# Linear attention followed by an MLP on one core: centring with the norm weight folded elsewhere, and matmuls on zeros in planned gaps of TensorE

## The chip, the cores and the metric

The kernel runs on one core of a Trainium2 chip. The metric is device time in microseconds (us) of one execution; lower is better. Four timed runs of the kernel before gave a median of 379.74 us (379.36 to 380.61). A core has the engines TensorE (PE: matmuls and weight loads), VectorE (DVE), ScalarE (ACT), GpSimd (POOL), and queues that issue transfers; SyncE (SP) here only issues transfers. Each engine works through its own instructions in order and waits at the head of its queue. Matmul results land in PSUM, of which this kernel uses eight banks.

## The reference

Shapes: q, k, v are 8 batches x 8 heads x 576 rows x 64 columns; w_phi is 64 x 128; the MLP is 512 -> 2048 -> 512.

```python
def phi(x):
    proj = np.einsum('bhsd,df->bhsf', x, w_phi)
    proj = proj - np.max(np.abs(proj), axis=-1, keepdims=True)
    return np.concatenate([np.exp(proj), np.exp(-proj)], axis=-1)
q_p, k_p = phi(q), phi(k)
kv = np.einsum('bhsf,bhsd->bhfd', k_p, v)
z = np.sum(k_p, axis=2)
num = np.einsum('bhsf,bhfd->bhsd', q_p, kv)
den = np.einsum('bhsf,bhf->bhs', q_p, z)[..., None] + 1e-06
# then, with the heads joined to x of 8 x 576 x 512:
mu = np.mean(x, axis=-1, keepdims=True)
var = np.mean((x - mu) ** 2, axis=-1, keepdims=True)
xn = (x - mu) / np.sqrt(var + 1e-06) * g_ln
out = x + np.maximum(xn @ w_ch1, 0.0) @ w_ch2
```

The MLP has no bias and a ReLU, so the positive factor 1/sqrt(var) of a row can be applied after the second matmul, and the kernel does that.

## The kernel before

The eight batches are four pairs. A pair has 1152 rows: nine tiles of 128 rows, in three groups r = 0, 1, 2 of three tiles. Attention runs in 32 units of two (batch, head) combinations, eight units a pair. In pair 0 units 0 to 3 finish batch 0 and units 4 to 7 batch 1; group r = 0 needs units 0 to 3 only.

One unit on the engines: transposes of k and q (L542; for later pairs a DMA transpose, L524), products with w_phi (`pm`, L572), row maxima on DVE (`m`, L592), exponentials on ACT (`EB`, L623), the product for the transposed features of q (`pt`, L670) with its exponentials (`ea`, L676), scaling of v on POOL (`vv`, L637 to L646), the sums over rows (`kv`, L696 and L701), numerator and denominator (`num`, L730), their scaling on DVE (L736 to L748) and the division on POOL, which writes the MLP's input x (L754).

The MLP for a group: row statistics on DVE (L873, L874), centring to `xc` (L881 on DVE, or the two steps L887 and L891 on POOL), a transpose to `xT` (pair 0: twelve TensorE transposes at L938, copied out of PSUM by L948; later pairs: DMA transposes, L923), the first matmuls (`hT_ps`, L989, four of 384 columns for each of 16 slices of 128 hidden columns), ReLU on ACT or DVE (L999, L997), the second matmuls (`ch_ps`, L1021), and scaling plus residual on DVE (L1029). The first `ch_ps` of pair 0 waits for all of w2.

Nothing of the order is fixed by loops. `Order` holds every operation with a rank, an estimated duration on each engine that may do it, what it reads and writes, and the PSUM banks it takes. `due` works backwards for due times; `run` simulates the engines with these estimates, gives each operation to an engine, and emits it into that engine's instruction list in that order. A change of a duration or of the allowed engines can thus reorder everything.

Two queues matter below. SP issues, in order, the loads of q, k, v and of g_ln; for pair 1 they begin with the row remainders `kx`, ahead of which POOL clears one small column (`kx1` memset, L1181), and all later loads of q, k and v stand behind these. POOL issues the loads of w1 and w2, two at a time, each pair of loads after the `vv` of units 2, 3, 5 and 6 (`WEIGHTS`, L1154).

Of the kernel before, what the change touches and what calls it, by code (L numbers as in the profile page):

```python
# [24 lines left out]


STAY = 10.0


class Op:  # L30
    __slots__ = (
        "alts", "emit", "rank", "lag", "users", "acquire", "release",
        "ready", "left", "number", "rows", "taken", "at", "early",
    )


class Order:
# [73 lines left out]
    def run(self):  # L111
        waiting, free, room, events, done = {}, {}, self.room, [], []
        rows = False

        def offer(op):
            heapq.heappush(events, (op.ready, 1, op.number, op, None))

        for op in self.ops:
            for engine in op.alts:
                waiting.setdefault(engine, [])  # L120
                free.setdefault(engine, 0.0)
            if not op.left:
                offer(op)
        now = 0.0
        while events:
            now = events[0][0]
            while events and events[0][0] <= now + 1e-9:
                _, kind, _, op, _ = heapq.heappop(events)
                if kind == 1:
                    for engine in op.alts:  # L130
                        key = op.ready if engine in ("DMA", "CAST") else op.rank
                        heapq.heappush(waiting[engine], (key, op.number, op))
                elif kind == 0:
                    for name, n in op.release or ():
                        room[name] += n
            for engine, queue in waiting.items():
                if free[engine] > now + 1e-9 or not queue:
                    continue
                passed, held, op = [], set(), None
                if engine == "PE" and rows:  # L140
                    near = sorted(i for i in queue if i[2].rows and not i[2].taken)
                    near = [i for i in near if room[i[2].acquire[0]] >= i[2].acquire[1]]
                    if near and near[0][0] < queue[0][0] + STAY:
                        op = near[0][2]
                while queue and op is None:
                    item = heapq.heappop(queue)
                    op = item[2]
                    if op.taken:
                        op = None
                        continue  # L150
                    if op.acquire is None or (
                        op.acquire[0] not in held and room[op.acquire[0]] >= op.acquire[1]
                    ):
                        break
                    held.add(op.acquire[0])
                    passed.append(item)
                    op = None
                for item in passed:
                    heapq.heappush(queue, item)
                if op is None:  # L160
                    continue
                op.taken, op.at = True, (now, engine)
                if op.acquire:
                    room[op.acquire[0]] -= op.acquire[1]
                us = op.alts[engine]
                if engine == "DMA" and free.get("CAST", 0.0) > now:
                    shared = free["CAST"] - now
                    us = 4.0 * us if 4.0 * us <= shared else us + shared * 0.75
                end = now + us
                if engine == "PE" and op.rows != rows:  # L170
                    rows = op.rows
                    end += 0.1
                lag = LAG[engine] if op.lag is None else op.lag
                free[engine] = end
                done.append((op, engine))
                heapq.heappush(events, (end, 2, op.number, op, None))
                heapq.heappush(events, (end + lag, 0, op.number, op, None))
                for o in op.users:
                    same = len(o.alts) == 1 and engine in o.alts
                    o.ready = max(o.ready, end + (0.1 if same else lag))  # L180
                    o.left -= 1
                    if not o.left:
                        offer(o)
        assert len(done) == len(self.ops)
        for op, engine in done:
            if op.emit:
                op.emit(engine)
        return now

# [2 lines left out]
def kernel(  # L192
# [45 lines left out]
    ps_B = ctx.enter_context(tc.tile_pool(name="ps_B", bufs=8, space=bass.MemoryType.PSUM))  # L238

    wphi_f = consts.tile([P, F], FP32, name="wphi_f")  # L240
    gln_sb = consts.tile([P, DM], FP32, name="gln")
    ident = consts.tile([P, P], BF16, name="ident")
    wbq = consts.tile([P, 2, F], BF16, name="wbq")
    wbk = consts.tile([P, 2, F], BF16, name="wbk")
    eps_sb = consts.tile([P, 1], FP32, name="eps")
# [32 lines left out]
    def add_any(alts, rank, emit, **kw):  # L278
        ahead_of = early(kw)
        sched.add(alts, rank, emit, early=ahead_of, **kw)  # L280

    def mm(n, cols):
        return n * (cols / 2.4 + 3.5) / 1000.0
# [102 lines left out]
    def load_w2(n, rank, after):  # L386
# [4 lines left out]
            r=after, w=[("w2", jj) for jj in range(j0, j1)],  # L391
        )

    def tails(g, V, qheads, with_k, slot):
# [19 lines left out]
        def products():  # L416
            pool, tag, _ = bank(g)
            j["px"] = ps = pool.tile([P, 1024 if tag == "A" else 512], FP32, tag=tag, name="px")
            for i, what in enumerate(parts):
                nc.tensor.matmul(  # L420
                    ps[:, i * 2 * F : (i + 1) * 2 * F], j["T"][:, i * P : (i + 1) * P],
                    wbk if what == "k" else wbq, start=True, stop=True,
                )
# [139 lines left out]
    def a_main(u, V, sides):  # L563
        n, g = u["n"], u["g"]

        def products(i):
            for e in range(2):
                u["pm", i, e] = ps_B.tile([P, MX // 2, F], FP32, tag="B", name="pm")
            for c in range(4):
                for e in range(2):  # L570
                    rows = slice(e * D, (e + 1) * D)
# [89 lines left out]
    def a_feat(u, V):  # L661
        n = u["n"]

        def products():
            u["EA"] = ea_bufs[n % NE]
            for e in range(2):
                u["pt", e] = ps_B.tile([P, 512], FP32, tag="B", name="pt")
            for e in range(2):
                rows = slice(e * D, (e + 1) * D)
                nc.tensor.matmul(  # L670
# [17 lines left out]
    def a_kv(u, V):  # L688
        n, g, uu = u["n"], u["g"], u["uu"]

        def products(t):
            EB, vv = u["EB"], u["vv"]
            if t == 1:
                u["kv"] = ps_B.tile([P, 2, 2, D1], FP32, tag="B", name="kv")
            ps = u["kv"]
            nc.tensor.matmul(  # L696
                ps[:, t, :, :], u["EBx"][:, t, uu, :], vv[:, t, MX : MX + 2, :],
# [20 lines left out]
    def a_num(u, V, chunks, em_of, puts, r):  # L718
# [4 lines left out]

        def products():
            st["ps"] = ps = ps_B.tile([P, 2, nch, D1], FP32, tag="B", name="num")
            for t in range(2):
                for i, terms in enumerate(chunks):
                    terms = terms(t)
# [133 lines left out]
    def x_stats(pr, r, V):  # L862
# [4 lines left out]
        for i, t in enumerate(ts):  # L867
# [8 lines left out]
            def center(e, i=i, t=t):  # L876
                if ("xc", r) not in pr:
                    pr["xc", r] = moe_sb.tile([P, NM, DM], BF16, tag="xc", name="xc")
                xc = pr["xc", r][:, i, :]
                if e == "DVE":  # L880
                    nc.vector.scalar_tensor_tensor(  # L881
                        out=xc, in0=x[:, t, :], scalar=pr["mv"][:, t, 0:1],
                        in1=gln_sb, op0=ALU.subtract, op1=ALU.mult,
                    )
                else:
                    xd = moe_sb.tile([P, DM], FP32, tag="xd", name="xd", bufs=1)
                    nc.gpsimd.tensor_tensor(  # L887
                        out=xd, in0=x[:, t, :], in1=bcast(pr["mv"][:, t, 0], 1, DM),
                        op=ALU.subtract,
                    )  # L890
                    nc.gpsimd.tensor_tensor(out=xc, in0=xd, in1=gln_sb, op=ALU.mult)  # L891

            w = [("mv", pair % 2, t)]
            if r == 0 and i == 0:
                w = [("mv", pair % 2, i_) for i_ in range(NT)]
            add("DVE", 0.72, V, stats, r=[("x", pair % NX, t, h) for h in range(H)], w=w)
            add_any({"DVE": 0.62, "POOL": 2.1}, V, center, r=["gln"] + [("mv", pair % 2, t)] + [("x", pair % NX, t, h) for h in range(H)],
                    w=[("xc", slot, i)])
            V += 1.0

# [9 lines left out]
    def x_trans(pr, r, slot_c, V):  # L910
# [20 lines left out]
        for k0 in range(0, KC, 2):  # L931
# [11 lines left out]
            def copy(e, k0=k0, st=st):  # L943
                if ("xT", r) not in pr:
                    pr["xT", r] = moe_sb.tile(
                        [P, KC, RN], BF16, tag="xT", name="xT", bufs=NXT
                    )
                copy_on(  # L948
                    e, pr["xT", r][:, k0 : k0 + 2, 0:cols],
                    st["ps"][:, 0 : 2 * cols].rearrange("p (k n) -> p k n", k=2),  # L950
                )

            key = ("xT_ps", pr["pair"], r, k0)
            wk = [("xT", slot, k0, i) for i in range(NM)]
            add("PE", mm(2 * n, 128), V, products, r=[("xc", slot_c, i) for i in range(n)],
                w=[key, *wk], acquire=("B", 1))
            add_any({"DVE": 0.08 + 0.128 * n, "ACT": 0.12 + 0.21 * n}, V, copy, r=[key], w=wk,
                    release=[("B", 1)])


# [17 lines left out]
    def moe(pr, V):  # L978
# [4 lines left out]
        def first(r, jj, V):  # L983
            st, cols = {}, len(tiles[r]) * P

            def products():
                st["ps"] = ps_B.tile([P, RN], FP32, tag="B", name="hT_ps")
                for kc in range(KC):
                    nc.tensor.matmul(  # L989
                        st["ps"][:, 0:cols], w1_sb[:, kc, jj * P : (jj + 1) * P],  # L990
# [133 lines left out]

    make_identity(nc, ident)
    nc.scalar.preload_act_table_set("natural_log_exp_and_others")
    for t_ in (wbk, wbq):
        nc.vector.memset(t_, 0.0)
    nc.vector.memset(eps_sb, 1e-6)
    for vx in vx_bufs:  # L1130
        nc.gpsimd.memset(vx, 0.0)
# [10 lines left out]
    for e_ in range(2):  # L1142
        add("DVE", 0.4, 0.0, lambda e=e_: phi_blocks(e), r=[("wphi", e_)], w=["wb"])

    dma("SP", 3.0, 262144, gln_sb, dram(moe_g_ln, 0, [[0, P], [1, DM]]), w=["gln"])
    load_main(k, 2, [0, 1], "SP", 3.0)
    load_main(q, 2, [0, 1], "SP", 3.1)
    load_tails(k, 0, [1], "SP", 3.2)
# [6 lines left out]
    for n in range(NU + 2):  # L1155
# [51 lines left out]
        if 0 < n <= NU:  # L1207
# [11 lines left out]
            if i == H - 1:  # L1219
                pr["V"] = V + 0.9 * step  # L1220
                ahead[0] = E_MOE
                moe_V = moe(pr, moe_V)
            ahead[0] = E_ATT
        gs = []
        if n % HG == 1 and n // HG + 3 != NGRP:
# [46 lines left out]
```

## Time and profile before

| What | us |
|---|---|
| median of the timed runs | 379.74 |
| the profiled execution's own time | 382.27 |
| span of its instructions | 380.5 |
| PE busy | 350.5 |
| DVE busy | 274.8 |
| ACT busy | 251.9 |
| POOL busy | 207.8 |
| first matmuls L989, x768 | 150.3 |
| second matmuls L1021, x551 recorded | 141.4 |
| centring: L881 on DVE x19 | 20.2 |
| centring: L887 + L891 on POOL x17 | 18.8 + 22.7 |
| load of g_ln: issued at 11.97, landed at | 19.54 |

The profile page gives busy times of each engine and the span in 40 slices of 9.5 us, each with a digit for the busy tenths. The row PEclk is the share of TensorE's full clock that was granted. Its records begin at 23.43 us; ahead of that the row shows full clock for want of a record. A window row lists, for one stretch, the busy time and the number of instructions of PE, PE weight loads, DVE, ACT and POOL, then the granted clock, the DMA share and GB/s. A timeline row gives start and duration, the engine, line and tiles, the number of merged instructions, and in brackets the idle time before it and what ended it. Matmuls overlap in the pipeline, so a row's duration holds the drain of its last matmul.

### The profile page before, as it was taken

The page shows a single profiled execution, that of the slowest core. Times are in us where ns is not written, and L with a number is a line of the kernel's source. Part 1 is how long each engine was busy: PE and PEld are TensorE (multiplying, and loading weights), DVE is VectorE, ACT ScalarE, POOL GpSimd, SP SyncE. Part 2 cuts the span into 40 slices and gives each one's busy share as a digit, 9 for nine tenths or more (in the row PEclk, how much of TensorE's full clock was granted, in tenths as well). Part 3 has the DMA queues.
Part 4 walks back from the last instruction along what each step waited for, and adds up shares of the span by engine and source line. Part 5 has one row for each costly group of instructions (what it writes and reads, how often), then busy time and mean ns, then how long its engine had stood idle before and what let it go on. Part 6 is the DMA issues. An engine that isn't in the chain of part 4 may idle for free.

```text
span 380.5 us, 9056 instructions
## 1 busy us (share of the span) xinstructions
PE 350.5 (92%) x3307; PEld 209.1 (55%) x3348; DVE 274.8 (72%) x723; ACT 251.9 (66%) x640; POOL 207.8 (55%) x368
## 2 busy tenths in 40 slices
PE   3877589999999999999999999999999999999995
PEld 1456366546665555555556555555566545555553
DVE  2878989799879779877879999976768886000102
ACT  3997669798889737886589557977779307433310
POOL 5588759889757668875446647853546432000000
PEclk9996669999999999999999999999999999999998
DMA  6899999978968953477556742712200125110102
GB/s 173 266 230 250 161 260 285 258 178 164 240 180 222 198 153 75 93 179 201 181 146 158 221 98 71 179 29 58 58 28 29 44 85 109 28 57 28 54 32 83
DMA packets 88749, 52.70 MB, mean 139 GB/s; under 512 B 55040, under 2 KB 84096, under 8 KB 88704
## 3 DMA queue, kind: packets, MB, share of 16 engines
q1 hardware_dynamic: 83856, 47.37, 49.5%
q0 software_dynamic: 4224, 4.19, 6.8%
q8 instruction: 26, 0.43, 0.5%
q10 hardware_dynamic: 624, 0.56, 0.5%
q14 instruction: 19, 0.16, 0.1%
HBM read 37.03 MB, written 9.44 MB: 122 GB/s over the span
## 4 chain that ended last, share of the span: by engine, by line
PE 64%; ACT 5%; DVE 4%; POOL 2%; issue 1%; DVEq 0%; POOLq 0%; DMA 0%
PE hT_ps L989 27%; PE ch_ps L1021 26%; PE num L730 3%; PE kv L701 3%; ACT ea L676 2%; PE pm L572 2%; ACT EB L623 2%; DVE m L592 1%; PE pt L670 1%; DVE st L873 1%; ACT hT L999 1%; PE kv L696 1%; POOL xc L891 1%; POOL xd L887 1%; DVE xc L881 1%
## 5 line engine op out<-in xcount | busy, mean ns | idle before, releaser
L989 PE MATMUL hT_ps<-xT,w 128*128 128x384 bf16 x768 | 150.3, 327 | 1.1 <-ACT EB L623 0.7
L1021 PE MATMUL ch_ps<-w,hT 128*128 128x512 bf16 (+2 forms) x551 | 141.4, 373 | 2.3 <-issue 0.5
L999 ACT ACTIVATE hT<-hT_ps 128x384 bf16<-128x384 f32 x130 | 64.0, 502 | 63.3 <-PE hT_ps L989 63.1
L989 PEld LDWEIGHTS <-w 128*128 128x128 bf16 x768 | 71.3, 98 | 54.5 <-issue 4.1
L592 DVE TENSOR_REDUCE m<-pm 128x4 f32<-128x512 f32 x128 | 82.1, 678 | 8.1 <-PE pm L572 7.8
L754 POOL TENSOR_TENSOR x<-numc,rden 128x192 bf16<-128x192 f32 (+1 forms) x112 | 50.6, 463 | 58.7 <-DVE rden L748 56.7
L1021 PEld LDWEIGHTS <-hT 128*128 128x128 bf16 x592 | 53.0, 98 | 45.8 <-issue 1.0
L623 ACT ACTIVATE EB<-pm 128x512 bf16<-128x512 f32 x128 | 68.4, 628 | 6.6 <-DVE m L592 4.5
L676 ACT ACTIVATE ea<-pt 128x512 bf16<-128x512 f32 x128 | 67.7, 628 | 7.4 <-PE pt L670 7.4
L1029 DVE SCALAR_TENSOR_TENSOR o<-ch_ps,rstd,x 128x512 f32<-128x512 f32 (+2 forms) x37 | 26.6, 726 | 54.1 <-PE ch_ps L1021 42.4
L637 POOL TENSOR_TENSOR vv<-v,emk 128x512 bf16<-128x512 f32 x32 | 33.5, 1047 | 37.2 <-ACT emk L608 23.6
L736 DVE TENSOR_TENSOR numc<-num,emq 128x195 f32<-128x195 f32 (+1 forms) x96 | 32.5, 344 | 20.8 <-PE num L730 16.9
L730 PEld LDWEIGHTS <-ea 128*128 128x128 bf16 x512 | 28.6, 101 | 15.8 <-issue 3.4
L997 DVE TENSOR_SCALAR hT<-hT_ps 128x384 bf16<-128x384 f32 x62 | 32.8, 540 | 2.7 <-PE hT_ps L989 2.4
L730 PE MATMUL num<-KV,ea 128*128 128x65 bf16 x512 | 32.4, 199 | 2.2 <-ACT EB L623 1.3
L742 DVE TENSOR_TENSOR numc<-numc,num 128x195 f32<-128x195 f32 (+1 forms) x100 | 33.4, 342 | 0.7
L637 POOL TENSOR_TENSOR vv<-v,en 128x512 bf16<-128x512 f32 x32 | 33.4, 1044 | 0.0
L873 DVE BATCH_NORM_STATS2 st<-x 128x6 f32<-128x512 bf16 x36 | 24.3, 674 | 4.2 <-POOL x L754 3.9
L701 PE MATMUL kv<-vv,EB 128*128 128x65 bf16 x512 | 25.9, 203 | 0.0
L572 PEld LDWEIGHTS <-qkT 64*128 64x128 bf16 x512 | 17.6, 101 | 12.8 <-issue 6.0
L701 PEld LDWEIGHTS <-EB 128*128 128x128 bf16 x512 | 23.4, 104 | 2.0 <-issue 0.3
L887 POOL TENSOR_TENSOR xd<-x,mv 128x512 f32<-128x512 bf16 x17 | 18.8, 1105 | 9.9 <-DVE mv L874 8.2
(67 smaller groups left out, 390.4 us busy)
## 6 DMA issues: line engine op xcount, KB each, us to landing
out_dram<-o SPq DMA_DIRECT2D x31, 256.0 KB, 2.4
qk<-in_k_dram SPq DMA_DIRECT2D x28, 256.0 KB, 4.9
v<-in_v_dram SPq DMA_DIRECT2D x28, 256.0 KB, 3.8
qk<-in_q_dram SPq DMA_DIRECT2D x26, 256.0 KB, 5.1
w<-in_moe_w_ch_dram POOLq DMA_DIRECT2D x8, 512.0 KB, 8.7
qk<-in_k_dram SPq DMA_DIRECT2D x2, 512.0 KB, 7.2
qk<-in_q_dram SPq DMA_DIRECT2D x2, 512.0 KB, 11.3
v<-in_v_dram SPq DMA_DIRECT2D x2, 512.0 KB, 10.8
```

Source lines behind the costliest of these rows:

```text
L592: nc.vector.reduce_max(out=u["m", i].rearrange("p (c e) -> p e c", e=2)[:, e], in_=u["pm", i, e], axis=AX.X, apply_absolute_value=True,)
L623: nc.scalar.activation(u["EB"][:, t, e * 4 : (e + 1) * 4].rearrange("p c f -> p (c f)"), u["pm", 1, e].rearrange("p c f -> p (c f)"), AF.E ...
L637: nc.gpsimd.tensor_tensor(out=u["vv"][:, t, 0:MX, 0:D], in0=vb[:, uu, :].rearrange("p (c d) -> p c d", d=D), in1=bcast(e[:, 0:MX], 2, D), ...
L676: nc.scalar.activation(u["EA"][:, t, e * 512 : (e + 1) * 512], u["pt", e], AF.Exp, scale=(1.0, -1.0)[t],)
L701: nc.tensor.matmul(ps[:, t, c // 4, :], EB[:, t, (c % 2) * 4 + c // 2, :], vv[:, t, c, :], start=False, stop=(t == 0 and c == MX - 1), ski ...
L730: nc.tensor.matmul(ps[:, t, i, :], lhsT, rhs, start=(j == 0), stop=(j == len(terms) - 1))
L742: nc.vector.tensor_add(out=st["numc"][:, 0:nch], in0=st["numc"][:, 0:nch], in1=st["ps"][:, 0])
L754: nc.gpsimd.tensor_tensor(out=dst, in0=st["numc"][:, i : i + cnt, 0:D], in1=bcast(st["rden"][:, i : i + cnt], 2, D), op=ALU.mult,)
L989: nc.tensor.matmul(st["ps"][:, 0:cols], w1_sb[:, kc, jj * P : (jj + 1) * P], pr["xT", r][:, kc, 0:cols], start=(kc == 0), stop=(kc == KC - 1),
L997: nc.vector.tensor_relu(h_sb[:, 0:cols], st["ps"][:, 0:cols])
L999: nc.scalar.activation(h_sb[:, 0:cols], st["ps"][:, 0:cols], AF.Relu)
L1021: nc.tensor.matmul(ch[t, c0], hT[r, jj][:, rt * P : (rt + 1) * P], w2_sb[:, jj, c0:c1], start=(jj == 0), stop=(jj == JC - 1),)
```

## The change

1. g_ln is loaded as 128 x 4 values (one per row of a transposed tile) instead of 128 rows x 512, and negated by one small DVE instruction.
2. Centring has one tensor input and makes mean - x, without g_ln: one instruction on DVE, ACT or POOL.
3. In pair 0 the copies of `xT` out of PSUM multiply by -g_ln: two of 128x384 instead of one of 128x768, twelve instead of six.
4. After pair 0, w1 is multiplied in place by -g_ln, 16 DVE instructions of 128x512, so that later pairs need no factor.
5. A tile of zeros is made first on DVE, and TensorE begins with ten matmuls of 256 columns on it.
6. For operations that the planner places before 60 us of its own time, six kinds of TensorE work are preceded by int(gap x 0.6 / 0.11) matmuls of 256 columns on zeros, where gap is TensorE's idle time ahead of them in the plan. They write to the bank that the work proper then overwrites.

```diff
+WARM = 60.0
@@ Order.run
+                op.gap = now - free[engine]
...
+                self.gap = op.gap if op.at[0] < WARM else 0.0
                 op.emit(engine)
@@
-    gln_sb = consts.tile([P, DM], FP32, name="gln")
+    gln_sb = consts.tile([P, KC], FP32, name="gln")
+    zeros = consts.tile([P, 256], BF16, name="zeros")
...
+    FILL = 0.6
+
+    def fill(ps, rows=slice(0, P)):
+        for _ in range(int(sched.gap * FILL / 0.11)):
+            nc.tensor.matmul(ps, zeros[rows, 0:P], zeros[rows, 0:256], start=True, stop=True)
...
+    def scale_w1(n, rank):
+        def emit():
+            for kc in range(KC):
+                w = w1_sb[:, kc, n * WC : (n + 1) * WC]
+                nc.vector.tensor_scalar_mul(out=w, in0=w, scalar1=gln_sb[:, kc : kc + 1])
+
+        add("DVE", 0.9, rank, emit, r=["gln"], w=[("w1", n, kc) for kc in range(KC)])
@@ tails (px), a_main (pm), a_feat (pt), a_kv (kv), a_num (num), first (hT_ps): after the bank is taken
+            fill(ps[:, 0:256])
@@ x_stats, center
-                if e == "DVE":
-                    nc.vector.scalar_tensor_tensor(
-                        out=xc, in0=x[:, t, :], scalar=pr["mv"][:, t, 0:1],
-                        in1=gln_sb, op0=ALU.subtract, op1=ALU.mult,
+                mean = pr["mv"][:, t, 0:1]
+                if e == "ACT":
+                    nc.scalar.activation(xc, x[:, t, :], AF.Identity, bias=mean, scale=-1.0)
+                elif e == "DVE":
+                    nc.vector.tensor_scalar(
+                        out=xc, in0=x[:, t, :], scalar1=-1.0, scalar2=mean,
+                        op0=ALU.mult, op1=ALU.add,
                     )
                 else:
-                    xd = moe_sb.tile([P, DM], FP32, tag="xd", name="xd", bufs=1)
                     nc.gpsimd.tensor_tensor(
-                        out=xd, in0=x[:, t, :], in1=bcast(pr["mv"][:, t, 0], 1, DM),
+                        out=xc, in0=bcast(pr["mv"][:, t, 0], 1, DM), in1=x[:, t, :],
                         op=ALU.subtract,
                     )
-                    nc.gpsimd.tensor_tensor(out=xc, in0=xd, in1=gln_sb, op=ALU.mult)
...
-            add_any({"DVE": 0.62, "POOL": 2.1}, V, center, r=["gln"] + [("mv", pair % 2, t)] + ...
+            add_any({"DVE": 0.35, "ACT": 0.5, "POOL": 1.05}, V, center, r=[("mv", pair % 2, t)] + ...
@@ x_trans, copy
-                copy_on(
-                    e, pr["xT", r][:, k0 : k0 + 2, 0:cols],
-                    st["ps"][:, 0 : 2 * cols].rearrange("p (k n) -> p k n", k=2),
-                )
+                for kk in range(2):
+                    dst = pr["xT", r][:, k0 + kk, 0:cols]
+                    src, g_ = st["ps"][:, kk * cols : (kk + 1) * cols], gln_sb[:, k0 + kk : k0 + kk + 1]
+                    if e == "ACT":
+                        nc.scalar.activation(dst, src, AF.Copy, scale=g_)
+                    else:
+                        nc.vector.tensor_scalar_mul(out=dst, in0=src, scalar1=g_)
...
-            add_any({"DVE": 0.08 + 0.128 * n, "ACT": 0.12 + 0.21 * n}, V, copy, r=[key], w=wk,
+            add_any({"DVE": 0.14 + 0.14 * n, "ACT": 0.14 + 0.21 * n}, V, copy, r=[key, "gln"], w=wk,
@@ set-up
-    for t_ in (wbk, wbq):
+    for t_ in (zeros, wbk, wbq):
         nc.vector.memset(t_, 0.0)
+
+    def warm_up():
+        ps = ps_B.tile([P, 256], FP32, tag="B", name="warm")
+        for _ in range(10):
+            nc.tensor.matmul(ps, zeros[:, 0:P], zeros, start=True, stop=True)
+
+    add("PE", 2.0, 0.0, warm_up, w=["warm"], acquire=("B", 1), release=[("B", 1)])
...
-    dma("SP", 3.0, 262144, gln_sb, dram(moe_g_ln, 0, [[0, P], [1, DM]]), w=["gln"])
+    dma("SP", 3.0, 20000, gln_sb, moe_g_ln.rearrange("(kc p) -> p kc", p=P), w=["gln"])
+    add("DVE", 0.1, 3.0, lambda: nc.vector.tensor_scalar_mul(out=gln_sb, in0=gln_sb, scalar1=-1.0),
+        w=["gln"])
@@ main loop, after moe(pr, moe_V)
+                if w_["pair"] == 0:
+                    for i_ in range(NW):
+                        scale_w1(i_, moe_V)
```

In the instruction lists of the two programs: TensorE gets 69 matmuls on zeros beside the ten at the start (ahead of `pm` 25, `pt` 24, `px` 11, `num` 4, `kv` 3, `hT_ps` 2), and its other work stands in nearly the same order. Centring goes from 19 DVE and 17 POOL (two steps each) to 3 DVE, 19 ACT and 14 POOL (one step each). ReLU goes from 62 DVE and 130 ACT to 73 DVE and 119 ACT. Of the twelve `xT` copies eight are on DVE and four on ACT. For group r = 0 of pair 0 two centrings are on POOL, one on DVE, and the two on POOL stand ahead of the `kx1` memset.

More of the change, by code (lines that the diff above doesn't have):

```diff
@@ L32 @@
         "alts", "emit", "rank", "lag", "users", "acquire", "release",
-        "ready", "left", "number", "rows", "taken", "at", "early",
+        "ready", "left", "number", "rows", "taken", "at", "early", "gap",
     )
@@ L568, in products @@
                 u["pm", i, e] = ps_B.tile([P, MX // 2, F], FP32, tag="B", name="pm")
+            fill(u["pm", i, 0][:, 0:2, :], slice(0, D))
             for c in range(4):
@@ L667, in products @@
                 u["pt", e] = ps_B.tile([P, 512], FP32, tag="B", name="pt")
+            fill(u["pt", 0][:, 0:256], slice(0, D))
             for e in range(2):
@@ L694, in products @@
                 u["kv"] = ps_B.tile([P, 2, 2, D1], FP32, tag="B", name="kv")
+                fill(u["kv"].rearrange("p t b d -> p (t b d)")[:, 0:256])
             ps = u["kv"]
@@ L725, in products @@
             st["ps"] = ps = ps_B.tile([P, 2, nch, D1], FP32, tag="B", name="num")
+            fill(ps.rearrange("p t c d -> p (t c d)")[:, 0:256])
             for t in range(2):
@@ L896, in x_stats @@
             add("DVE", 0.72, V, stats, r=[("x", pair % NX, t, h) for h in range(H)], w=w)
-            add_any({"DVE": 0.62, "POOL": 2.1}, V, center, r=["gln"] + [("mv", pair % 2, t)] + [("x", pair % NX, t, h) for h in range(H)],
+            add_any({"DVE": 0.35, "ACT": 0.5, "POOL": 1.05}, V, center, r=[("mv", pair % 2, t)] + [("x", pair % NX, t, h) for h in range(H)],
                     w=[("xc", slot, i)])
@@ L987, in products @@
                 st["ps"] = ps_B.tile([P, RN], FP32, tag="B", name="hT_ps")
+                fill(st["ps"][:, 0:256])
                 for kc in range(KC):
```

## Prediction

> **What bounds the kernel now.** First the slices of the page (9.5 us each), to see where TensorE is not full and where its clock falls.
>
> ```profile
> PE   3877589999999999999999999999999999999995
> DVE  2878989799879779877879999976768886000102
> PEclk9996669999999999999999999999999999999998
> ```
>
> TensorE is full from the seventh slice on. Then the windows that cut the span there:
>
> ```profile
> 0.00:60.00 60.00, 41.20 (x487) 28.27 (x488) 46.82 (x139) 43.53 (x115) 41.06 (x91) 0.83 0.98 229
> 60.00:85.00 25.00, 23.86 (x234) 13.96 (x234) 22.39 (x64) 21.55 (x58) 22.58 (x37) 1.00 1.05 233
> 85.00:380.50 295.50, 285.45 (x2588) 166.90 (x2626) 205.58 (x523) 186.84 (x470) 144.18 (x242) 1.00 0.45 112
> ```
>
> TensorE idles 18.8 us in the first 60 and 10.1 us after 85, of which 4.7 follow its last matmul (375.8). So from 85 on the time is TensorE's own work, which the change leaves as it is; after 85 the waits of TensorE that the profile names add up to 3.7 us. What can move the end is how early the MLP's work becomes ready, and that is settled in the first 75 us, on three things: DVE (46.8 of 60, and full from 30 to 44), transfers, and the clock.
>
> For the clock I cut the first 60 us at its steps. The records change at 23.43, 30.26, 37.09, 40.50 and 54.15, all whole multiples of 3.41 us apart.
>
> ```profile
> 16.60:20.02 3.42, 2.94 (x31) 1.58 (x30) 2.99 (x6) 3.42 (x12) 3.42 (x8) 1.00 0.87 301
> 20.02:23.43 3.41, 3.41 (x58) 3.03 (x57) 2.26 (x6) 2.78 (x8) 2.79 (x6) 1.00 1.18 266
> 26.84:30.26 3.42, 1.60 (x27) 1.25 (x27) 1.75 (x8) 3.42 (x10) 2.51 (x7) 1.00 1.12 249
> 37.09:40.50 3.41, 2.15 (x29) 1.25 (x26) 3.41 (x14) 3.41 (x10) 3.41 (x9) 1.00 1.23 212
> 50.74:54.15 3.41, 3.41 (x29) 2.10 (x27) 2.66 (x7) 2.01 (x6) 1.82 (x5) 0.50 1.19 229
> ```
>
> And the timeline, for what a matmul takes in each state and where TensorE waits:
>
> ```profile
> 19.51 0.65 PE L701 MATMUL kv<-vv,EB 128*128 128x65 bf16 x8
> 25.11 0.22 PE L410 MATMUL xT_ps<-ident,kx 128*128 128x128 bf16 x1 [0.74 <-DMA kx<-in_k_dram]
> 42.55 2.11 DVE L881 SCALAR_TENSOR_TENSOR xc<-x,mv,gln 128x512 bf16<-128x512 bf16 x1
> 46.19 1.38 DVE L881 SCALAR_TENSOR_TENSOR xc<-x,mv,gln 128x512 bf16<-128x512 bf16 x2
> 48.43 1.46 PE L938 MATMUL xT_ps<-ident,xc 128*128 128x128 bf16 x12 [3.26 <-DVE numc L742]
> 51.65 1.49 PE L989 MATMUL hT_ps<-xT,w 128*128 128x384 bf16 x4
> 54.26 0.81 PE L989 MATMUL hT_ps<-xT,w 128*128 128x384 bf16 x4
> 63.92 0.42 PE L701 MATMUL kv<-vv,EB 128*128 128x65 bf16 x8
> ```
>
> Eight `kv` matmuls take 0.65 us at 19.51, where the page shows full clock for want of a record, and 0.42 at 63.92: TensorE ran at half clock until 23.43. In all it was slow for 23.4 + 6.8 + 13.7 = 43.9 us. The clock rose after windows with 3.41, 3.36 (33.67 to 37.09) and 3.41 us of PE busy and not after 2.94 or 3.00 (9.78 to 13.19); it fell after 1.60 and 2.15 and not after 2.42 (23.43 to 26.84). The limits lie between.
>
> **The change part by part.**
>
> *The load of g_ln.* It is the 262 KB load that landed at 19.54, by the landing events 2.2 us after the one ahead of it; the loads behind it are those that TensorE waits for (`kx` 0.74 at 25.11, `qx` 1.7 at 29.02). The Trainium skill (DMA: Bandwidth & Descriptors, Rules for kernel authors) speaks against the new form: a strided last dimension becomes one descriptor for each element, here 512 of 4 bytes. The nearest row is the `kx` remainder, 256 pieces of 256 bytes, which lands 0.2 to 0.3 us after its neighbour; twice that is 0.4 to 0.7. By the row later loads come 1.5 us sooner; by the rule alone, with each piece as dear as a long one, nothing is won. I take -1.0, bounds -1.7 and +0.5. The small DVE multiply now waits for this load and has the row maxima and numerators of units 0 and 1 behind it; DVE gets to that place at 20.2 (its L630), about 1 us after the landing, so it costs its 0.1.
>
> *Centring of r = 0.* DVE has next to no idle time from 42.4 to 48.6, and TensorE waits 3.26 us for it. It drops three L881 (2.11 + 1.38 = 3.5) and one 128x768 copy (0.56). It gets one single-input centring, bounded by the 128x512 copy out of PSUM (0.40) and by 0.15, at 0.35, and four `xT` copies at about 0.36 (half of 0.56 is 0.28; the 128x512 copy 0.40): +1.8. On the path -2.2, bounds -2.9 and -1.3. The two POOL centrings, 1.1 each by L887, fall where POOL is idle (45.6 to 48.8), if nothing waits behind them: see below.
>
> *Centring of r = 1 and 2.* TensorE waited 0.8 us, until 73.95, for POOL's second step (L891, 1.27). Without that step -0.7.
>
> *The clock.* A zero matmul of 256 columns costs two thirds of one of 384: at half clock four of these take 1.49, of which 0.32 each in a stream, so 0.21; at full clock 0.11. The ten at the start take 2.1 us from about 1.1 to 3.3 and end ahead of the first landing (3.70): hidden. They don't fill a window, so they raise nothing. Of the 69 others 26 stand ahead of what ran by 20 us: 5.5 us over four windows that had 2.3 to 3.0 busy. That fills one of them, and the clock rises some 5 to 10 us sooner. The 43 others add 43 x 0.11 = 4.6 us over eleven windows, 0.4 each: 2.15 becomes 2.57 and holds, 1.60 becomes 2.0 and still falls. Slow time then is about 25 us. Only where TensorE was full does this shorten the path: 20.02 to 23.43 (but `kx` and ACT end the next waits, so 0) and 50.74 to 54.15, where half of 3.41 is won: -1.7; 33.67 to 37.09 lies under a full DVE. Here too a rule stands apart from the rows: TensorE: Matmul & The Clock Gate (Why this matters for your kernels) asks for at least 4 us of continuous work to get the clock and no gap over about 3 us to keep it. By it the drop at 30.26, which no gap over 1.9 us preceded, would not be there, one broken gap (44.97 to 48.43) would be enough, and the second half of the trace's slow time would go, about -3.4. I go by the rows. Bounds 0 (zeros don't count as work) and -4.
>
> *What the fills cost.* They can't start until the bank is theirs, and many gaps of TensorE before 60 end with an exponential that gives a bank back (0.48 at 18.91, 0.37 at 40.00, 0.36 at 58.42). There the fill doesn't use the gap but follows it: eight ahead of the third `pt` are 1.7 us at half clock. All 69 are 14.7 us slow, 7.4 fast. Most wait for an operand, or lie under DVE or ACT; if a tenth of the mean comes through, +1.0. Bounds 0 and +7.
>
> *POOL and SP.* Both POOL centrings now stand ahead of the `kx1` memset, and wait for DVE's statistics of r = 0. SP's wait for that memset is there already:
>
> ```profile
> SPq L300 <- POOL kx L1181: 13.1, 1, 13.1
> ```
>
> Behind it SP holds all loads of q, k and v for pair 1, and behind it on POOL are `vv` of unit 5 and the third pair of weight loads. By the durations (statistics 3 x 0.86, two centrings 2.2) the memset moves from 40.5 to about 44. Late next is w2: its last part landed at 68.7, the first `ch_ps` was at 71.1, so the cover is 2.4 us, and transfers are at their limit from 47 to 68. The 3.9 us won ahead of that point (1.0 + 2.2 + 1.7 - 1.0) would use it up. I let 2.4 be given back there: +2.4, bounds 0 and +5.
>
> *Later pairs.* POOL loses 26 us, DVE 16 centrings of 0.77 or more, ACT gains about 12 us of centring by its 0.63 for 512 elements and gives eleven ReLUs of 0.5 to DVE. TensorE's named waits there are 3.7 us; a third goes: -1.2, bounds -3.5 and +2. The scaling of w1 (16 x 0.35 = 5.6 us of DVE between about 110 and 150) has the 48 second matmuls of the last group (three take 0.65, so 10 us) as cover ahead of pair 1's first use; the DVE in that stretch is at 33 of 40: +0.3.
>
> **The sum**: -1.0 - 2.2 - 0.7 - 1.7 + 1.0 + 2.4 - 1.2 + 0.3 = -3.1 us, against the profiled execution's 382.3, so 379.2; its span is 380.5. That execution stood 2.5 above the median of the timed runs, so I give 379.7 - 3.1 = 376.6.
>
> **The rivals.**
> 1. *The fills are on the path* (slower). For it: the waits for banks above; the planner knows only full clock, so at half clock 60% of a gap becomes 120%. Against: DVE, not TensorE, is full from 30 to 44. Half of the 69 at half clock are +7.4 in place of +1.0: -3.1 + 6.4 = +3.3, 383.0. It decides once more than 4 us of fills show up as later starts of `EB` and `ea`.
> 2. *w2 is not late.* The last part is issued behind `vv` of unit 6 (57.75), and if it and the loads ahead of it move up with the rest, nothing is given back: -5.5; with the drops of the clock gone (-1.7 more), -7.2: about 373.
> 3. *Hidden anyway.* The early units are bound by ACT (43.5 of 60), transfers and w2, and all that DVE and the clock win ends in those waits: within 1 us of 379.7.
> 4. *Zeros don't count as work* for the clock: the change doesn't do what its second half is for, +1.7 to +2.7 on the sum, about 379.
>
> **How the numbers follow.** Forecast (376.6, with 374.5 to 378.5 as its own range) 0.42; rival 2 0.17; rivals 3 and 4 together 0.11; rival 1, with the moved memset at its bound of +5 counted in, 0.30. About 0.3% (1.1 us) is what a measurement of this kernel tells from no change. Faster: 0.42 + 0.17 + 0.02 = 0.61; within: 0.08; slower: 0.31. The range has to take in rival 2 down to 371 and rival 1 up to 383.5.
>
> **What would show it.** Right: PEclk records that rise before 20 us and hold through 50 to 54; the first `hT_ps` about 2 us before 51.5; `xT_ps` no longer waiting 3 us for DVE; `kx` landing before 24. Wrong: `pt` and `pm` starting later than before by the length of their fills; the `kx1` memset at 46 or later with a wait of the first `ch_ps` for w2; DVE standing at the w1 scaling for a matmul.

## The result, and the profile after

The changed kernel takes 378.03 us (median of 44 runs, 375.29 to 381.52); the kernel before, beside it, 379.92 (63 runs, 378.25 to 382.17). The ratio of the two is 0.9946, with a 95% interval of 0.9934 to 0.9958, or 2.05 us of 379.92: small, and clear of the noise. The forecast was 376.6. The profiled execution of the changed kernel has a span of 376.8 us and a time of 378.6, near its median; that of the kernel before (380.5 and 382.3) stood 2.3 us above its own. The 3.7 us between the spans therefore show more than the change is worth, and a difference below that rests on these two traces alone can be off by up to 1.7 us.

The slices of the page, 9.4 us each:

```profile
PE   6878899699999899999999999999999999999995
DVE  2899999779879999977879879978788672000111
PEclk9899999899999999999999999999999999999999
```

The clock row is no longer down between 28 and 57 us. It dips in the second slice and once more in the eighth. The windows with the earlier bounds (stretch and length; busy us of PE, PEld, DVE, ACT and POOL with their counts; granted clock, DMA share, GB/s):

```profile
0.00:60.00 60.00, 49.91 (x646) 34.82 (x647) 50.84 (x154) 48.82 (x132) 48.03 (x103) 0.97 0.98 218
60.00:85.00 25.00, 21.16 (x204) 12.12 (x205) 20.98 (x60) 17.32 (x47) 13.45 (x27) 0.93 1.17 264
85.00:376.80 291.80, 282.33 (x2540) 164.31 (x2577) 202.81 (x527) 190.66 (x474) 121.09 (x221) 1.00 0.45 112
```

TensorE is busier before 60 (49.9 us, the matmuls on zeros included, where it was 41.2) and less busy from 60 to 85 (21.2, where it was 23.9). Something was won early and part of it given back at once. The windows around the clock's two dips, on the grid of 3.41 us on which its records change:

```profile
7.67:11.08 3.41, 3.33 (x31) 2.03 (x29) 2.37 (x4) 1.74 (x5) 0.00 (x0) 1.00 0.59 135
11.08:14.49 3.41, 2.29 (x29) 1.38 (x29) 3.30 (x9) 3.41 (x12) 0.42 (x1) 1.00 0.96 274
14.49:17.91 3.42, 3.42 (x27) 2.21 (x26) 2.27 (x7) 3.42 (x10) 3.42 (x7) 0.50 0.90 275
69.10:72.52 3.42, 0.99 (x7) 0.26 (x6) 2.24 (x8) 1.17 (x4) 2.08 (x2) 1.00 1.07 109
72.52:75.94 3.42, 3.20 (x21) 1.65 (x23) 2.48 (x4) 3.42 (x7) 0.22 (x1) 0.50 1.12 345
```

The clock is full from 11.08 (the records begin there; what lies ahead was at half), half again from 14.49 to 17.91, full to 72.52, half to 75.94. Slow in all: 11.1 + 3.4 + 3.4 = 17.9 us, where the kernel before had 43.9. The timeline shows the first MLP work, and the place where the lead ends:

```profile
41.60 0.83 PE L962 MATMUL xT_ps<-ident,xc 128*128 128x128 bf16 x12 [0.59 <-ACT ea L697]
67.78 0.79 PE L962 MATMUL xT_ps<-ident,xc 128*128 128x128 bf16 x11 [0.56 <-DVE xc L907]
68.62 1.46 PE L1049 MATMUL ch_ps<-w,hT 128*128 128x512 bf16 x6
72.51 0.61 PE L592 MATMUL pm<-wbk,qkT 64*128 64x128 bf16 x8 [2.43 <-DMA qkT<-qkb]
```

The transposes of r = 0 start at 41.60 instead of 48.43 and wait 0.59 us for an exponential instead of 3.26 for DVE. At 72.51 TensorE has stood 2.43 us for the eighth unit's `qkT`. The kernel before had no such wait. In the chain that ended last the same step stands as

```profile
61.65 10.81 DMA qkT<-qkb
72.46 0.05 issue
72.51 1.03 PE pm L592 x13
```

The DMA transpose was issued at 61.65 and landed at 72.46; the loads queued ahead of it (`k`, `q` and `v` of group six) landed until 70.16. In the kernel before it was issued at 64.93, when the last of these had landed (64.16), and landed at 69.75.

Counting matmuls of the same kind in the traces gives the lead along the way, with two of the experiments beside (us from each span's start). The 65th, 129th and 193rd `hT_ps` begin the next groups of rows. Other work between two points is not quite the same in all columns: between the first and the 65th stand 54 matmuls named `kv` in the changed kernel and 36 in the kernel before, so a step of about 1 us from one row to the next says little by itself.

| point in TensorE's work | before | after | no zeros | zeros only |
|---|---|---|---|---|
| first transposes of r = 0 | 48.43 | 41.60 | 42.10 | 46.71 |
| first `hT_ps` | 51.65 | 44.37 | 44.93 | 50.76 |
| 57th `hT_ps` | 69.35 | 62.33 | 63.35 | 68.55 |
| first `ch_ps` | 71.11 | 64.44 | 65.46 | 70.31 |
| 65th `hT_ps` | 81.95 | 79.45 | 76.92 | 81.10 |
| 129th `hT_ps` | 105.33 | 102.98 | 102.19 | 104.48 |
| 193rd `hT_ps` | 146.92 | 146.53 | 145.74 | 146.06 |
| 384th `hT_ps` | 217.54 | 216.54 | 214.95 | 216.69 |
| 513th `hT_ps` | 275.00 | 270.70 | 269.10 | 274.15 |
| 768th `hT_ps` | 366.76 | 363.76 | 362.16 | 366.56 |
| span | 380.5 | 376.8 | 375.2 | 379.6 |

So the changed kernel is 7.3 us ahead at the first `hT_ps`, 2.5 at the 65th, only 0.4 at the 193rd, 1.0 at the 384th, 4.3 at the 513th and 3.7 at the end. The early lead is nearly all given back, and most of what is left at the end is won behind the 384th. From there to the end of the span it takes 162.92 us before and 160.29 after. The same stretch takes 162.92 with zeros only and 160.27 without zeros, so this gain goes with the rest of the change and not with the zeros. In the waits of TensorE from 215 to 275 us (waiter, releaser, us in all, times, longest) the kernel before has five entries, 1.9 us together, of which the two longest are

```profile
PE pm L572 <- DVE numc L742: 0.7, 1, 0.7
PE xT_ps L410 <- ACT ea L676: 0.5, 1, 0.5
```

and the changed kernel has one:

```profile
PE ch_ps L1049 <- issue: 0.5, 3, 0.2
```

### The profile page after: what moved, and what is told of

It reads as the page before. It is cut to its first block, busy times and chain, and to the rows that moved or that the text cites. A ratio compares the mean times of both kernels' runs of the same rounds, so it can differ in the third digit from the quotient of the medians.

```text
span 376.8 us, 9229 instructions
## 1 busy us (share of the span) xinstructions
PE 353.4 (94%) x3385; PEld 211.2 (56%) x3427; DVE 274.6 (73%) x739; ACT 256.8 (68%) x650; POOL 182.6 (48%) x349
## 4 chain that ended last, share of the span: by engine, by line
PE 72%; DMA 10%; DVE 8%; ACT 5%; issue 2%; POOL 1%; SPq 0%; DVEq 0%; POOLq 0%
PE ch_ps L1049 30%; PE hT_ps L1017 28%; DMA qkT<-qkb 4%; DMA qk<-in_q_dram 4%; PE pm L592 4%; PE num L753 4%; PE kv L723 3%; DVE m L612 2%; ACT ea L697 2%; DMA v<-in_v_dram 2%; PE pt L691 1%; DVE numc L759 1%; ACT EB L643 1%; DVE numc L765 1%; PE kv L718 1%
## 5 line engine op out<-in xcount | busy, mean ns | idle before, releaser
L1027 ACT ACTIVATE hT<-hT_ps 128x384 bf16<-128x384 f32 x119 | 58.5, 498 | 57.3 <-PE hT_ps L1017 57.0
L697 ACT ACTIVATE ea<-pt 128x512 bf16<-128x512 f32 x128 | 69.0, 637 | 7.9 <-PE pt L691 7.7
L643 ACT ACTIVATE EB<-pm 128x512 bf16<-128x512 f32 x128 | 69.2, 636 | 2.7 <-DVE m L612 2.2
L1025 DVE TENSOR_SCALAR hT<-hT_ps 128x384 bf16<-128x384 f32 x73 | 39.0, 543 | 4.9 <-PE hT_ps L1017 4.3
L753 PEld LDWEIGHTS <-ea 128*128 128x128 bf16 x512 | 27.5, 98 | 12.9 <-issue 1.1
L753 PE MATMUL num<-KV,ea 128*128 128x65 bf16 x512 | 31.2, 194 | 0.4 <-ACT ea L697 0.2
L592 PEld LDWEIGHTS <-qkT 64*128 64x128 bf16 x512 | 17.9, 97 | 15.5 <-issue 7.4
L905 ACT ACTIVATE xc<-x,mv 128x512 bf16<-128x512 bf16 x19 | 13.8, 725 | 14.8 <-DVE mv L897 12.4
L723 PE MATMUL kv<-vv,EB 128*128 128x65 bf16 x512 | 23.5, 194 | 0.0
L723 PEld LDWEIGHTS <-EB 128*128 128x128 bf16 x512 | 21.1, 98 | 1.5
```

Source lines behind the costliest of these rows:

```text
L643: nc.scalar.activation(u["EB"][:, t, e * 4 : (e + 1) * 4].rearrange("p c f -> p (c f)"), u["pm", 1, e].rearrange("p c f -> p (c f)"), AF.E ...
L697: nc.scalar.activation(u["EA"][:, t, e * 512 : (e + 1) * 512], u["pt", e], AF.Exp, scale=(1.0, -1.0)[t],)
L723: nc.tensor.matmul(ps[:, t, c // 4, :], EB[:, t, (c % 2) * 4 + c // 2, :], vv[:, t, c, :], start=False, stop=(t == 0 and c == MX - 1), ski ...
L753: nc.tensor.matmul(ps[:, t, i, :], lhsT, rhs, start=(j == 0), stop=(j == len(terms) - 1))
L1025: nc.vector.tensor_relu(h_sb[:, 0:cols], st["ps"][:, 0:cols])
L1027: nc.scalar.activation(h_sb[:, 0:cols], st["ps"][:, 0:cols], AF.Relu)
```

## The experiments

From this table came theory T: transfers set the end of the first pair, the wait at 72.5 eats the lead, and an earlier `qkT` would bring it back. The rivals were that the zeros carry the gain (Z), that the centring alone does (C), and that the zeros stand in the way (F). Every ratio below is to the kernel before, timed on the same chip (380.42 us median there).

**No zeros.** The burst of ten and all fills are left out; the order of the other work is that of the changed kernel.

```
-    FILL = 0.6
+    FILL = 0.0
-    add("PE", 2.0, 0.0, warm_up, w=["warm"], ...)
+    add("PE", 2.0, 0.0, None, w=["warm"], ...)
```

> The changed kernel with all 79 zero matmuls left out and the plan as it was. Theory T (a transfer sets the end of the first pair): the zeros bring the work up to the first ch_ps some 4 us forward, and the centring with the smaller load the other 2 to 3 us; but the first pair then waits for the eighth unit's qkT, which lands at 72 us, so without zeros PE's wait of 2.4 us there goes and little is lost: first ch_ps at 67 to 69 us instead of 64.4, and in all 0 to 1 us slower than the changed kernel (ratio to the kernel before 0.994 to 0.998). Rival Z (the zeros' clock carries the gain): 2 us or more slower than the changed kernel, a ratio of 1.000 or more. Rival F (the zeros stand in the way of real work): faster than the changed kernel, a ratio under 0.993.

Measured: 377.24 us, ratio 0.9918 (0.9895 to 0.9941). That is 0.0028 below the changed kernel's ratio; the two intervals together give 1.1 us faster, give or take 1.0. By the numbers set ahead this is rival F; the upper end of the interval just reaches T's 0.994, and Z is out. The clock did lose what the zeros had won. Windows without zeros:

```profile
25.73:29.14 3.41, 1.64 (x27) 1.12 (x27) 3.08 (x15) 3.41 (x11) 3.39 (x8) 1.00 0.96 226
29.14:32.55 3.41, 3.19 (x31) 2.19 (x30) 3.41 (x13) 3.38 (x11) 3.30 (x9) 0.50 1.18 246
35.97:39.38 3.41, 1.97 (x19) 0.86 (x17) 3.38 (x11) 3.18 (x8) 3.19 (x8) 1.00 1.24 205
42.80:46.21 3.41, 3.41 (x31) 2.23 (x30) 3.38 (x15) 0.86 (x4) 2.88 (x6) 0.50 0.80 181
```

The clock was at half to 22.31, from 29.14 to 32.55 and from 39.38 to 46.21: 32.6 us in all, 14.7 more than with the zeros. In all four windows DVE was full or nearly so (3.08 to 3.41 of 3.41). In the first and the third TensorE itself stood idle for 1.4 to 1.8 us; in the second and the fourth both were busy nearly throughout, TensorE at half clock. That DVE set the pace there is likely; no run tests it. The timeline without zeros:

```profile
42.10 1.44 PE L962 MATMUL xT_ps<-ident,xc 128*128 128x128 bf16 x12 [0.47 <-ACT ea L697]
71.38 0.40 PE L592 MATMUL pm<-wbk,qkT 64*128 64x128 bf16 x8 [0.28 <-DMA qkT<-qkb]
```

Twelve transposes take 1.44 us at half clock and 0.83 at full, and yet they start only 0.5 us later, and the first `hT_ps` 0.56 later. Ahead of the first `hT_ps` TensorE was at half clock for 31.3 us without zeros and for 14.5 with them, and 0.56 us is all that this was worth there, net of the time that the zeros themselves took; at the 57th `hT_ps` it is 1.0. At the transfer, TensorE comes 1.0 us later and `qkT` 1.1 earlier (71.33; it was issued at 61.55, as late as with the zeros), so the wait is 0.28 instead of 2.43, and the clock does not fall behind it. By the 65th `hT_ps` this kernel is 2.5 us ahead of the one with zeros; 0.8 of that is left at the 129th, and 1.6 at the end.

**Zeros only.** The kernel before, with the zeros tile, the burst of ten and the fills (72 of them here, since the plan's gaps are its own); centring, copies, g_ln and w1 as before. The edit, shortened:

```
+    zeros = consts.tile([P, 256], BF16, name="zeros")
+    FILL = 0.6
+    add("PE", 2.0, 0.0, warm_up, w=["warm"], ...)
+            fill(ps[:, 0:256])        # and in the other five places
```

> The kernel before with the zeros tile, the burst of ten and the zero matmuls in the planned gaps; centring, copies, load of g_ln and w1 as before. Theory T: the clock comes up some 20 us earlier than before, first ch_ps at 66 to 68 us (71.1 before), which is about where the wait for the eighth unit's qkT begins to bite; 1 to 2.5 us faster than before (ratio 0.993 to 0.997). Rival C (the gain is the centring's alone): ratio 0.999 to 1.002. Rival F (the zeros cost more than the clock brings): over 1.002.

Measured: 381.30 us, ratio 1.0022 (1.0002 to 1.0041): 0.8 us slower, give or take 0.7. Against T, and on the border of C and F. In the timeline the wait of the transposes for DVE is nearly what it was in the kernel before (3.26):

```profile
46.71 1.46 PE L953 MATMUL xT_ps<-ident,xc 128*128 128x128 bf16 x12 [3.09 <-DVE numc L757]
```

The clock was full from 19.00 to 39.48 instead of from 23.43 with a gap, and was at half twice more before 53.13. Over all timed runs its mean rose from 0.981 to 0.991. The trace has TensorE 0.9 us ahead at the first `hT_ps` and at every later row of the table but the last `hT_ps` (0.2); from the first to the end of the span it is 328.85 us against 328.82. So nothing behind the first `hT_ps` changed. The 0.9 us cannot be set against the 0.8 us of the timed runs, since the profiled execution of the kernel before was one of its longer ones.

The two comparisons agree: with the new centring or with the old one, the zeros cost. Weighted by their intervals: +0.9 us, give or take 0.6. And both say the same of everything else in the change: -3.1 us (ratio 0.9918), or, the changed kernel against zeros only, 0.9946 - 1.0022 = -0.0076, -2.9 us, each give or take 0.9. In the traces 2.6 us of this lie behind the 384th `hT_ps`, as shown above. An estimate from these figures is therefore that all that was won and lost ahead of it, from the first centring to the scaling of w1, is worth 0.3 to 0.5 us, give or take 0.9.

**The large load put back.** The changed kernel with the 262 KB broadcast load of g_ln issued ahead of the small one, into a tile that nothing reads (the edit without the tile's own line).

```
+            if dst is gln_sb:
+                eng.dma_start(out=gbig, in_=dram(moe_g_ln, 0, [[0, P], [1, DM]]))
```

> The changed kernel with the old 262 KB load of g_ln issued as well, just ahead of the small one, into a tile that nothing reads. Theory T: what is queued behind it lands 1 to 2 us later up to 30 us, the first ch_ps comes 0.5 to 1.5 us later than 64.4, and the qkT of the eighth unit also lands up to 1 us later since the queue is without gap to 72 us: 0 to 0.8 us slower than the changed kernel (ratio 0.994 to 0.997). Rival L (the load is worth its 1.0 us or more on the path): ratio 0.9975 or more.

Measured: 378.41 us, ratio 0.9933 (0.9907 to 0.9960). The load costs nothing that can be seen: 0.5 us less than the changed kernel, give or take 1.1, so at most 0.6 more. Rival L is out. The large load landed at 18.24, only 0.79 us after the load ahead of it, and the small one 0.19 later. The remainder loads of `kx` behind them landed at 22.45 and 22.73 (21.48 and 23.11 in the changed kernel), the first `hT_ps` came at 44.80 (44.37). The wait at the transfer is there again, and longer (the waits of TensorE from 60 to 85: waiter, releaser, us in all, times, longest):

```profile
PE pm L595 <- DMA qkT<-qkb: 3.0, 1, 3.0
PE pm L595 <- ACT ea L700: 0.2, 1, 0.2
```

**The transposes ahead of the loads.** The changed kernel with the loads of group six issued behind the first two DMA transposes of `qkb` (the edit, shortened).

```
+        if n == 5:
+            gs.remove(5)
+        if n == 7:
+            gs = [5] + gs
-                    load_main(t_, g_, [0, 1], "SP", V + 0.5 + 0.1 * i_)
+                    load_main(t_, g_, [0, 1], "SP", V + 0.5 + 0.1 * i_, [("turn", 8)] if g_ == 5 else [])
```

> The changed kernel with the loads of the sixth group of k, q and v issued behind the first two DMA transposes of qkb instead of ahead of them; nothing else is changed by hand. Theory T: the eighth unit's qkT then lands by 68 us instead of 72.5, PE's wait of 2.4 us and the slow clock window of 72.5 to 75.9 us go, and the lead of 6.7 us at the first ch_ps is kept to 80 us but for 1 us or so: 2 to 4 us faster than the changed kernel (ratio 0.984 to 0.990). Rival B (the lead is lost to bandwidth or to PE's own work by 150 us whatever stands first, since after 150 us the changed kernel was only 1 us ahead): ratio 0.992 to 0.996. Rival N (the delayed loads of k, q and v are then late themselves): over 0.997.

Measured: 378.89 us, ratio 0.9957 (0.9933 to 0.9980): 0.4 us slower than the changed kernel, give or take 1.0, where T asked for 2 to 4 us faster. T falls, and rival B's number fits; the interval also reaches into N's (over 0.997). The edit did what it should: `qkT` landed at 68.87 instead of 72.46, and no half-clock record follows. It still took 8.95 us from its issue at 59.92, with none of group six ahead of it, so these loads are not all that held it; the last part of w2 landed at 67.29. But the planner moved TensorE's work along with it, and the wait only came earlier:

```profile
68.92 0.40 PE L592 MATMUL pm<-wbk,qkT 64*128 64x128 bf16 x8 [2.16 <-DMA qkT<-qkb]
77.16 0.34 PE L753 MATMUL num<-KV,ea 128*128 128x65 bf16 x6 [0.86 <-DVE st L896]
```

Waits for DVE that the changed kernel did not have follow at 77.16. From the first `hT_ps` to the 129th it takes 58.39 us, the changed kernel 58.61. The lead is lost over that stretch whichever of its loads stands first; what this edit does not show is the stretch with no wait for `qkT` at all. The two traces don't start it level: this kernel's first `hT_ps` comes at 46.24, 1.9 us later than the changed kernel's, after a clock that was at half until 26.34, with the same 79 matmuls on zeros.

## Why the prediction was right or wrong

The sign and the range were right; the time was 1.4 us above the forecast and inside its own range. That it came so close is in part luck: the forecast had most of the gain won early, ahead of the first `ch_ps`, and the traces have nearly all of it behind the 384th `hT_ps`. Terms that were wrong in both directions cancelled.

*The clock, -1.7, and what the fills cost, +1.0.* Together -0.7 was predicted and +0.9 (give or take 0.6) measured: the one wrong sign in the sum. That zeros count as work for the clock was right: the mean granted clock of the timed runs was 0.993 with them (44 runs of the changed kernel) and 0.983 without (6 runs). Slow time fell to 17.9 us in the trace of the changed kernel, further than the 25 predicted, but that is one execution: the traces with the large load and with the transposes first, with the same zeros, have 22.4 and 26.3. The 43.9 of the old trace is high too, since its granted clock is 0.970 and those of 25 timed runs of that kernel 0.975 to 0.987.

The two terms together hold up to the 57th `hT_ps`, where the trace with zeros is 1.0 us ahead of the one without. The step that failed is that this would last to the end. Ahead of the first `hT_ps` the kernel without zeros was behind by 0.56 us only. TensorE then came earlier to a `qkT` that did not land earlier, waited 2.43 us, and lost its clock for 3.4 us. Against this, the zeros cost as much on the kernel before, where that wait does not exist. What the zeros cost there is open, and so is the share of the burst and of the fills in it; neither was tried alone.

Of rival 1 the direction was right, and its mechanism is hardly seen in the traces: `pm` of the first unit starts 1.33 us after its `q` lands with and without its four fills, and the batches of `pm`, `pt`, `kv` and `num` up to 42 us start between 0.5 us earlier and 1.2 us later than without zeros. The largest, a `pt` at 19.10 with six fills just ahead of it, is later by 1.16, but the `kv` behind it at 19.74 by 0.19 only. The `pm` at 7.75 and 17.10, later by 0.7 and 0.8, follow loads that landed 0.6 to 0.7 later.

*POOL and SP, +2.4 given back at w2.* That the lead is given back just after the first `ch_ps` was right; the place was wrong. The `kx1` memset did not move (SP behind it starts the loads at 40.96, before 40.65), since everything ahead of it had come forward too, and w2's last part landed at 67.58 without a wait for it. The first `ch_ps` had started at 64.44, ahead of that landing: it does not wait for all of w2, though the plan and the description above have it so, and the cover of 2.4 us was no limit. In place of w2 came the `qkT` transpose (2.43), a half-clock window behind it, and the xc of r = 1 (0.56). The amount was larger too: 4.8 us between the first `hT_ps` and the 65th with zeros, 1.7 without, the `kv` and `num` that moved ahead of the 65th included.

*Centring of r = 0, -2.2.* Mis-sized: without zeros the first `hT_ps` came 6.7 us sooner, since the wait of 3.26 for DVE went altogether and the units ahead moved forward with it. Of this 3.1 us stand at the 129th `hT_ps`, 1.2 at the 193rd and 2.6 at the 384th, in a pair of traces of which the old one was slow. Set against the trace with zeros only, which is near the median of its runs (381.42 and 381.30), the changed kernel is 6.4 us ahead at the first `hT_ps`, 1.5 at the 129th and 0.2 at the 384th. So the mechanism was right at its place, and next to nothing of it reached the end. *Centring of r = 1 and 2, -0.7*: TensorE still waits, 0.56 instead of 0.8 us, now for DVE's centring (the line at 67.78), so it brought 0.2.

*The load of g_ln, -1.0.* Wrong: the load put back costs at most 0.6 us and probably nothing. The 2.2 us after its neighbour, on which the row rested, were those of one trace; put back, the same load landed 0.79 us after the one ahead of it, while the small load took 0.72 in the changed kernel. The other reading, from the rule of the Trainium skill (DMA: Bandwidth & Descriptors, Rules for kernel authors) of one descriptor for each element, was that nothing is won. That came out for the time, but no run here shows that the 512 pieces were dear.

On the clock neither the limits read from the window rows nor the rule (TensorE: Matmul & The Clock Gate, Why this matters for your kernels) held. Against the rule, it fell at 14.49 after a window with 2.29 us busy and no gap over 0.5 us, and at 72.52 after a gap of under 3 us. Against the limits, two later windows of the same trace with no more work (2.02 and 2.27 us) kept it; the second is

```profile
28.15:31.56 3.41, 2.27 (x39) 1.88 (x38) 3.38 (x13) 3.41 (x11) 3.29 (x9) 1.00 1.17 244
```

and with the transposes first a full window did not raise it. Its records begin at 26.34, and behind the full window eight `kv` still take the 0.65 us of the half clock:

```profile
19.51:22.92 3.41, 3.41 (x36) 2.24 (x35) 1.47 (x6) 1.50 (x4) 3.04 (x6) 1.00 1.07 223
23.42 0.65 PE L723 MATMUL kv<-vv,EB 128*128 128x65 bf16 x8
```

*Later pairs, -1.2, and w1, +0.3.* Mis-sized both, in opposite directions. Behind the 384th `hT_ps` alone the changed kernel is 2.6 us quicker, with the zeros and without, twice the whole term. Of TensorE's waits that the profile names from 215 to 275 us, 1.4 us go (1.9 to 0.5). Whether that comes of ACT's taking the centring, of the step that POOL lost or of the new order of the plan was not tried apart. The scaling of w1 costs about 1.0 and not 0.3. The chain has four of its multiplications standing in front of a row maximum:

```profile
123.56 2.29 DVE w L408 x4
```

and in the waits of TensorE from 70 to 150 us the `hT_ps` behind that maximum is the second:

```profile
PE pm L592 <- DMA qkT<-qkb: 2.4, 1, 2.4
PE hT_ps L1017 <- DVE m L612: 1.0, 1, 1.0
```

The group is 16 multiplications of 478 ns instead of the 350 that were estimated. What the prediction overlooked is that DVE takes four in a row, so that a row maximum queued behind them is 2.3 us late. The cover of 10 us named there was for w1's readers, not for what else DVE owes.

The sum without the zeros' two terms was -2.4 and measured -3.1 (give or take 0.9); with them -3.1, measured -2.05. The total was nearer than its parts: the later pairs were to bring 1.2 us, and what stands behind the 384th `hT_ps` alone brought 2.6; the terms ahead of it were to bring 1.2 without the zeros (1.0 + 2.2 + 0.7 - 2.4 - 0.3), and 0.3 to 0.5, give or take 0.9, is left for them.

## What to carry to other kernels

In this kernel cheap work that kept TensorE's clock up did not pay, though the clock rose: ahead of spending instructions on it, look in each slow window at which other engine is full and at what the engine will meet next. A lead won early is worth what is left of it behind the next shared limit (here 0.4 us of 7.3 at the 193rd `hT_ps`), so read the change at several fixed points of the work, down to the end, and not at the first one that moved. One trace can be slow or lucky: set beside it a second one whose time is near its median. A part of a change that was meant to help should be taken out alone: here the version without the zeros is the fastest that was measured, 377.24 us.

## What the runs showed of the hardware that was not expected

A DMA transpose of a 128x1024 bf16 tile took 10.81 us from issue to landing behind loads that were already queued, 4.82 in the kernel before and 8.95 with the transposes first, on the same queue. No limit on the busy time of one window, as the prediction worked it out from the first trace, fits the clock of all traces: it fell after 2.29 us and stayed after 2.02 and 2.27 in the same trace, stayed after 1.79 with the transposes first, rose after 3.19 in one kernel, and did not rise after 3.41 in two (19.51 to 22.92 with the transposes first, 12.17 to 15.59 with zeros only). A wait of 2.43 us was followed by a half clock in the changed kernel and a wait of 2.16 us with the transposes first was not. The steps all lie on a grid of 3.41 us whose place against the start of the kernel differs between the traces (a step at 11.08, 18.95 or 26.34 us with the same zeros); what decides at a step, the runs do not settle.
